# Expert 1's weight loads ahead of expert 2's transposing loads on one queue, and joins of an expert's planes tied behind VectorE's sums, in a fused attention and mixture-of-experts kernel

## The chip, the cores and the metric

The program runs on one core of one Trainium2 chip. The metric is the device time of one execution in microseconds (us), lower is better. The kernel before took 710.95 us, the median of three timed executions (710.29 to 711.34).

## What is computed

A gated linear recurrence over 768 steps (4 batches, 8 heads, head size 48) gives 3072 tokens of 384 numbers. A noisy gate picks two of eight experts for each token; an expert is two matrix products with a ReLU between them, weighted and added to the token's output row. All is in float32.

```python
def _moe_ref(x, w_gate, w_noise, noise, w1, w2):
    ...
    for e in range(E):                       # 8 experts
        for k in range(2):
            mask = top2[:, k] == e
            h = np.maximum(x[mask] @ w1[e], 0.0)                       # 384 -> 1024
            out[mask] += top2_w[mask, k, None] * (h @ w2[e])           # 1024 -> 384
```

## The kernel before, in words

The first 40% of the span is the attention, the gates and the dispatch of token rows to slots in DRAM (`xs`). The change lies behind that, in the experts, which run one after the other.

**One expert.** An expert has 832 slots, in two windows: window 0 with 320 rows (output blocks j = 0, 1, 2 of 128, 128 and 64 rows) and window 1 with 512 rows (blocks 3 to 6 of 128). Each float32 operand is held as two parts, high and low, and a product is three matmuls: high by high, high by low, low by high.

- `load_w1` and `load_w2` load the weights as three and four pieces into `raw` (three buffers, shared by both); ScalarE casts a piece to the high part (line 789), VectorE subtracts for the low part (line 790), and that frees the `raw` buffer.
- `load_x` loads the slots' rows into `xga` (window 0) and `xgb` (window 1); `x_G` takes the gate weights and the token numbers out of them.
- From expert 2 on, `x_P` splits the rows into 16-bit halves (ScalarE, line 754) and writes them to DRAM (`xp`, line 755); `x_L` reads them back with transposing DMAs (`xu`, line 763, six for a window); `x_T` joins the two halves of one of three planes again on VectorE (`xj`, line 828, the **join**), makes the high part on ScalarE (line 829) and the low part on VectorE (line 830). There are six joins for an expert, three for each window.
- `mm1` is the first product: eight blocks f for each window, nine matmuls each (line 842) into `ph`, which has four accumulator banks. ScalarE's ReLU gives the high part of `h` (line 844), VectorE the low part (line 847); in window 0 that is two instructions, of 256 and 64 columns. When both are done the bank is free.
- `mm2` is the second product: 24 matmuls for an output block (line 868; the 64-row block j = 2 has eight and eight, lines 873 and 876) into `po`, which has **two** accumulator banks. VectorE's **sum** (line 881) multiplies by the gate weight and adds into `ao`, and so frees the bank; a GpSimd DMA scatters `ao` to the output (line 882). `gather_o` fetches the output rows of the next expert into `ao`.

**What sets the order.** Up to the end of expert 1 each engine's and the sync queue's order (SP) is written out by hand in `ORDER`, tokens like `load_w21.2` (piece 2 of expert 1's second weights), `x_L2_0.3` (expert 2, window 0, transposing load 3), `mm21_1_4.0` (expert 1, output block 4: VectorE's sum) and `x_T2_1_0.0` and `.1` (expert 2, window 1, plane 0: join and low part). Of the experts from 2 on, the loop at the end emits the calls, and a scheduler places them on the engines by priority and its own estimate; SP's DMAs alone are held in the order of the calls. In the loop the joins of the next expert stand behind `mm2(e, 0)` and `mm2(e, 1)` in the text, and the scheduler may move them ahead:

```python
        mm2(e, 0)
        if e + 1 < E:
            for kk in range(KD):
                x_T(e + 1, 0, kk)
        mm2(e, 1)
```

Of the kernel before, what the change touches and what calls it, by code (L numbers as in the profile page):

```python
# [13 lines left out]
U16 = mybir.dt.uint16  # L14
I32 = mybir.dt.int32
AF = mybir.ActivationFunctionType
OP = mybir.AluOpType
# [198 lines left out]
        load_w12.2 mm20_1_4.0 load_w12.1 mm11_1_1.0 x_G2_0.1 x_G2_0.0 load_w21.0 mm20_1_5.0 mm11_1_0.0 mm20_1_6.0  # L216
        load_w21.1 load_w21.3 load_w21.2 mm11_1_2.0 mm11_1_3.0 mm11_1_4.0 mm11_1_5.0 mm21_0_0.0 mm11_1_6.0 mm21_0_1.0
        mm11_1_7.0 x_T2_0_0.0 x_T2_0_0.1 x_G2_1.0 x_G2_1.1 mm21_0_2.0 mm21_0_2.1 x_T2_0_1.0 x_T2_0_1.1 x_T2_0_2.0
        x_T2_0_2.1 mm21_1_3.0 x_T2_1_0.0 x_T2_1_0.1 x_T2_1_1.0 x_T2_1_1.1 x_T2_1_2.0 x_T2_1_2.1 mm21_1_4.0 mm21_1_5.0
        mm21_1_6.0  # L220
    """,
    "SP": """
        load_a0.0 load_a0.1 load_a1.0 load_a1.1 load_a2.0 load_a2.1 load_qk0.0 load_qk1.0 load_a3.1 load_qk2.0 p31.0
# [15 lines left out]
        load_v20.0 load_v21.0 load_v22.0 p322.1 load_w20.0 load_w20.1 load_w20.2 gscat3_0_4.0 gscat4_0_3.0 load_x1_0.0  # L239
        load_w20.3 load_v23.0 load_x1_0.1 load_w11.0 load_w11.1 load_w11.2 gscat4_3_4.0 load_w12.0 gscat5_3_4.0  # L240
        gscat5_0_3.0 load_x0_1.0 load_w12.1 load_w12.2 load_x1_1.0 load_x2_0.0 clear_out3.0 load_x2_0.1 load_w21.0
        load_w21.1 load_x2_1.0 x_P2_0.0 x_L2_0.0 x_L2_0.1 x_L2_0.2 x_L2_0.3 x_L2_0.4 x_L2_0.5 load_w21.2 load_w21.3
        x_P2_1.0 x_L2_1.0 x_L2_1.1 x_L2_1.2 x_L2_1.3 x_L2_1.4 x_L2_1.5
    """,
}
# [74 lines left out]
def kernel(  # L320
# [8 lines left out]
    nc = tc.nc  # L329
# [5 lines left out]
    N, DM = out.shape  # L335
    E = w_gate.shape[1]
    FF = w1.shape[2]
    KD = DM // 128
# [9 lines left out]
    JS = ((0, 1, 2), (3, 4, 5, 6))  # L348
# [396 lines left out]
        return d  # L745

    XU = {}

    def x_P(e, w):
        js = JS[w]  # L750
# [36 lines left out]
    order = mybir.DependencyInfo(mybir.DependencyClass.NoSync, mybir.DependencyReason.DATA)  # L787
# [28 lines left out]
    def x_T(e, w, kk):  # L816
        n = WIN[w][1]
        src_t = xga if w == 0 else xgb
        js = JS[w]
        x = XW[w, kk] = mt([128, 2, n], F32R, name=f"x{w}{kk}")  # L820
        if e < 2:
            p = ps_tile("px")
            for j in js:
                o = TO[j]
                nc.tensor.transpose(p[:, o:o + 128], src_t[:, j - js[0], kk * 128:(kk + 1) * 128], ident)
        else:
            p = mt([128, 512], F32, name="xj")
            nc.vector.tensor_copy(p[:, :n].bitcast(U16).rearrange("p (d two) -> p two d", two=2), XU[w, kk])  # L828
        nc.scalar.copy(x[:, 0, :], p[:, :n])  # L829
        nc.vector.tensor_tensor(x[:, 1, :], p[:, :n], x[:, 0, :].bitcast(F32), op=OP.subtract)  # L830

# [23 lines left out]
                in_offset=bass.IndirectOffsetOnAxis(ap=OX[e][0:w, j:j + 1], axis=0),  # L855
                bounds_check=N - 1, oob_is_err=False)

    osc = {}

    def mm2(e, w, js=None):  # L860
        for j in js or JS[w]:
            n, o = TW[j], TO[j]
            p = psO.tile([128, 512], F32, name="po")
            a, g = ao[j][0:n, :], GW[e][0:n, j:j + 1]
# [5 lines left out]
            else:  # L870
# [7 lines left out]
                lo = mt([n, DM], F32, name="lo")  # L878
                nc.scalar.copy(lo, p[n:2 * n, :DM])
                nc.vector.scalar_tensor_tensor(a, lo, g, a, op0=OP.mult, op1=OP.add)  # L880
            nc.vector.scalar_tensor_tensor(a, p[0:n, :DM], g, a, op0=OP.mult, op1=OP.add)  # L881
            d = nc.gpsimd.indirect_dma_start(  # L882
                out=out, out_offset=bass.IndirectOffsetOnAxis(ap=OX[e][0:n, j:j + 1], axis=0),
                in_=a, in_offset=None, bounds_check=N - 1, oob_is_err=False)
# [9 lines left out]
    for g in range(NG):  # L894
# [12 lines left out]
        for j in range(B):  # L907
            n = B * g + j
# [111 lines left out]

    emit([c for x in sorted(fill) for c in fill[x]])

    after = mybir.DependencyInfo(mybir.DependencyClass.NoSync, mybir.DependencyReason.DATA)
    for i, (first, *rest) in sorted(phases.items()):
        for x in rest:
            tc.add_manual_dep(x.ins, first.ins.name, after, reason="table")
# [108 lines left out]
    for e in range(2, E):  # L1135
        if e == 3:
            flag = flags()
            held.close()
        load_w2(e)
        gather_o(e)  # L1140
        mm1(e, 0)
        if e + 1 < E:
            load_x(e + 1, 0, xga)
            load_x(e + 1, 1, xgb)
        mm1(e, 1)
        if e + 1 < E:
            load_w1(e + 1)
            for w in range(2):
                x_G(e + 1, w)
                x_P(e + 1, w)  # L1150
            for w in range(2):
                x_L(e + 1, w)
        mm2(e, 0)
        if e + 1 < E:
            for kk in range(KD):
                x_T(e + 1, 0, kk)
        mm2(e, 1)
        if e + 1 < E:
            for kk in range(KD):
                x_T(e + 1, 1, kk)  # L1160
    nc.pop_inst_callback()
    mctx.close()

# [168 lines left out]
```

## Time and profile before

| what | value |
|---|---|
| timed executions | 710.95 us median of 3 (710.29 to 711.34) |
| the profiled execution | 705.07 us |
| its span (first to last instruction) | 703.4 us |
| TensorE matmul busy | 671.9 us, 96% of the span |
| VectorE busy | 438.2 us, 62% |
| ScalarE busy | 359.6 us, 51% |
| TensorE's mean granted clock | 0.99 of full speed |

PE is TensorE's matmuls, PEld its weight loads, DVE VectorE, ACT ScalarE, POOL GpSimd, SP the sync queue. The profiled execution is 5.9 us shorter than the median of the timed ones. The time that an engine waits stands in brackets behind the instruction that ended the wait, with what released it; a line of the windows view gives the engines' busy time in a stretch and the clock that TensorE was granted there.

### The profile page before, as it was taken

To read this page: it belongs to the slowest core of one execution; us is meant where nothing else is said; L and a number is where in the kernel's file an instruction comes from. 1 tells how busy PE (TensorE), PEld (TensorE's weight loads), DVE (VectorE), ACT (ScalarE), POOL (GpSimd) and SP (SyncE) were. 2 spreads that over 40 slices of the span, in tenths; PEclk is the share of its full clock that TensorE was granted. 3 is DMA by queue.
4 is the path that set the end of the run, shared out by engine and by line. 5 is a ranking of instruction groups with operands and counts; after the bars stand their busy time and mean duration, and the time that the engine had idled before them with its cause. 6 is when DMAs were issued, how large, how long until landed. Compare 5 with 4: busy or idle time off the path is not lost.

```text
span 703.4 us, 14277 instructions
## 1 busy us (share of the span) xinstructions
PE 671.9 (96%) x5532; PEld 591.5 (84%) x5535; DVE 438.2 (62%) x985; ACT 359.6 (51%) x597; POOL 176.4 (25%) x187
## 2 busy tenths in 40 slices
PE   7999999999999999996999899999999999999995
PEld 2477787888888998895998898898899899899895
DVE  7999999999987573513566445535627626644321
ACT  6899999989655423414265135217317307403200
POOL 3000000443453320333142124124123122323221
PEclk9999999999999999998999999999999999999998
DMA  6857667766787361355466448528617727632110
GB/s 228 257 163 186 190 186 250 193 218 198 230 284 244 135 240 47 118 171 163 133 213 196 126 138 248 150 81 275 166 61 268 165 100 256 157 118 76 42 39 31
DMA packets 101916, 118.52 MB, mean 168 GB/s; under 512 B 58738, under 2 KB 81115, under 8 KB 101840
## 3 DMA queue, kind: packets, MB, share of 16 engines
q1 hardware_dynamic: 92288, 89.98, 42.0%
q0 software_dynamic: 9552, 27.54, 12.0%
q8 instruction: 46, 0.75, 0.4%
q14 instruction: 30, 0.25, 0.1%
HBM read 70.91 MB, written 40.34 MB: 158 GB/s over the span
## 4 chain that ended last, share of the span: by engine, by line
PE 46%; DMA 12%; SPq 10%; DVE 10%; ACT 9%; issue 3%; POOL 0%; POOLq 0%; ACTq 0%; DVEq 0%
PE po L868 19%; SPq L763 9%; PE ph L842 8%; DMA xgb<-xs 4%; PE ptr L565 3%; DMA xu<-xp 3%; PE psc L575 2%; DMA xp<-xp 2%; PE pY L624 2%; ACT xp L754 2%; PE pY L626 2%; PE po L873 2%; PE po L876 2%; PE psc L842 2%; ACT w1h L789 1%
## 5 line engine op out<-in xcount | busy, mean ns | idle before, releaser
L868 PE MATMUL po<-w2h,h 128*128 128x384 f32 x768 | 200.3, 337 | 6.2 <-ACT w2h L789 6.2
L842 PE MATMUL ph<-x,w1h 128*128 128x512 f32 (+1 forms) x720 | 194.1, 354 | 0.4 <-DVE h L847 0.4
L868 PEld LDWEIGHTS po<-w2h,h 128*128 128x128 f32 x768 | 140.3, 189 | 7.5 <-ACT w2h L789 6.6
L842 PEld LDWEIGHTS ph<-x,w1h 128*128 128x128 f32 x720 | 127.8, 188 | 16.5 <-ACT h L844 0.8
L868 PE MATMUL po<-w2l,h 128*128 128x384 f32 x384 | 129.4, 337 | 0.3 <-DVE w2l L790 0.3
L842 PE MATMUL ph<-x,w1l 128*128 128x512 f32 (+1 forms) x360 | 127.3, 354 | 0.2 <-DVE w1l L790 0.2
L882 POOL DMA_INDIRECT out_dram<-ao,ox x56 | 56.8, 1014 | 276.0 <-DVE ao L881 228.4
L847 DVE SCALAR_TENSOR_TENSOR h<-ph,h 128x512 fp32r<-128x512 f32 (+2 forms) x176 | 73.9, 451 | 57.9 <-ACT h L844 57.7
L844 ACT ACTIVATE h<-ph 128x512 fp32r<-128x512 f32 (+1 forms) x120 | 62.0, 525 | 76.1 <-PE ph L842 66.1
L699 POOL DMA_INDIRECT xs<-xr,sl x48 | 54.1, 1127 | 180.1 <-DMA v<-in_v_dram 118.4
L881 DVE SCALAR_TENSOR_TENSOR ao<-po,gw,ao 128x384 f32<-128x384 f32 (+1 forms) x56 | 33.9, 611 | 76.1 <-PE po L868 75.2
L842 PEld LDWEIGHTS ph<-x,w1l 128*128 128x128 f32 x360 | 67.6, 188 | 8.6 <-DVE w1l L790 0.5
L868 PEld LDWEIGHTS po<-w2l,h 128*128 128x128 f32 x384 | 72.6, 189 | 1.1 <-DVE w2l L790 0.7
L789 ACT CAST w2h<-raw 128x768 fp32r<-128x768 f32 x32 | 26.6, 834 | 87.4 <-PE po L868 70.5
L853 POOL DMA_INDIRECT ao<-out_dram,ox x49 | 57.4, 1171 | 52.4 <-issue 34.8
L829 ACT CAST x<-xj 128x320 fp32r<-128x320 f32 (+1 forms) x36 | 19.5, 540 | 67.3 <-DVE xj L828 67.3
L790 DVE TENSOR_TENSOR w2l<-raw,w2h 128x768 fp32r<-128x768 f32 x32 | 30.3, 956 | 25.2 <-ACT w2h L789 24.5
L575 PEld LDWEIGHTS psc<-qT,kT 112*64 112x64 f32 x768 | 36.4, 137 | 6.7 <-issue 2.8
L575 PE MATMUL psc<-qT,kT 112*64 112x128 f32 (+1 forms) x768 | 40.1, 250 | 1.8 <-DVE h L847 1.4
L828 DVE COPY xj<-xu 128x640 uint16<-128x640 uint16 (+1 forms) x36 | 23.2, 644 | 23.3 <-DMA xu<-xp 22.9
L626 PE MATMUL pY<-am,v 128*48 128x128 f32 x384 | 36.3, 274 | 0.3
L576 DVE TENSOR_TENSOR am<-psc,mask 128x512 f32<-128x512 f32 x48 | 32.5, 682 | 3.0 <-PE psc L575 2.9
(218 smaller groups left out, 1012.9 us busy)
## 6 DMA issues: line engine op xcount, KB each, us to landing
raw<-in_moe_w_dram SPq DMA_DIRECT2D x24, 512.0 KB
raw<-in_moe_w_dram SPq DMA_DIRECT2D x32, 384.0 KB
qk<-in_qk_dram SPq DMA_DIRECT2D x24, 384.0 KB
v<-in_v_dram SPq DMA_DIRECT2D x24, 288.0 KB
xgb<-xs SPq DMA_DIRECT2D x8, 800.0 KB
re<-in_a_dram SPq DMA_DIRECT2D x12, 384.0 KB
im<-in_a_dram SPq DMA_DIRECT2D x12, 384.0 KB
out_dram<-none SPq DMA_DIRECT2D x12, 384.0 KB
```

The lines of the kernel that those rows point to most:

```text
L575: nc.tensor.matmul(p[o:o + 64, j, z:], KT[n][:, h, z:z + 64], QT[n][:, h, z:], start=True, stop=True, skip_group_check=True)
L626: nc.tensor.matmul(o, V[n][:, H + h // 2 if h % 2 else h, :], AM[n][:, h, :], start=not g, stop=True, skip_group_check=True)
L699: d = nc.gpsimd.indirect_dma_start(out=xs, out_offset=bass.IndirectOffsetOnAxis(ap=sl[:, kk, b:b + 1], axis=0), in_=XR[g][:, lo + b, :], i ...
L763: nc.sync.dma_start(x[:, i, :], xp[e % 2, lo:lo + n, i * DM + kk * 128:i * DM + (kk + 1) * 128], transpose=True)
L789: nc.scalar.copy(hi, raw_t)
L842: nc.tensor.matmul(p[:, :n], W1[e, kk][i][:, f * 128:(f + 1) * 128], XW[w, kk][:, j, :], start=(m == 0), stop=(m == len(ms) - 1))
L844: nc.scalar.activation(h[:, 0:n], p[:, :n], AF.Relu)
L847: nc.vector.scalar_tensor_tensor(h[:, dst:dst + b - a], p[:, a:b], 0.0, h[:, a:b].bitcast(F32), op0=OP.max, op1=OP.subtract)
L853: nc.gpsimd.indirect_dma_start(out=ao[j][0:w, :], out_offset=None, in_=out, in_offset=bass.IndirectOffsetOnAxis(ap=OX[e][0:w, j:j + 1], ax ...
L868: nc.tensor.matmul(p[:, :DM], HT[w, f][i][:, o:o + 128], W2[f // 2][k2][:, f % 2, :], start=(m == 0), stop=(m == len(ms) - 1))
L881: nc.vector.scalar_tensor_tensor(a, p[0:n, :DM], g, a, op0=OP.mult, op1=OP.add)
L882: d = nc.gpsimd.indirect_dma_start(out=out, out_offset=bass.IndirectOffsetOnAxis(ap=OX[e][0:n, j:j + 1], axis=0), in_=a, in_offset=None, b ...
```

## The change

Three orders change; no operation is added or taken away.

1. On SP, `load_w21.2` and `load_w21.3` stand ahead of the six transposing loads `x_L2_0`, no longer behind them.
2. On VectorE, in the table, the sums of expert 1's output blocks 4, 5 and 6 stand between the joins of expert 2's window 1, no longer behind all three.
3. In the loop, each join of expert e + 1 is tied behind the sum that was emitted last: the first two joins behind block 3, the next two behind block 4, one behind block 5, one behind block 6.

```diff
     "DVE":
-        x_T2_0_2.1 mm21_1_3.0 x_T2_1_0.0 x_T2_1_0.1 x_T2_1_1.0 x_T2_1_1.1 x_T2_1_2.0 x_T2_1_2.1 mm21_1_4.0 mm21_1_5.0
-        mm21_1_6.0
+        x_T2_0_2.1 mm21_1_3.0 mm21_1_4.0 x_T2_1_0.0 x_T2_1_0.1 mm21_1_5.0 x_T2_1_1.0 x_T2_1_1.1 mm21_1_6.0 x_T2_1_2.0
+        x_T2_1_2.1
     "SP":
-        load_w21.1 load_x2_1.0 x_P2_0.0 x_L2_0.0 x_L2_0.1 x_L2_0.2 x_L2_0.3 x_L2_0.4 x_L2_0.5 load_w21.2 load_w21.3
+        load_w21.1 load_x2_1.0 x_P2_0.0 load_w21.2 load_w21.3 x_L2_0.0 x_L2_0.1 x_L2_0.2 x_L2_0.3 x_L2_0.4 x_L2_0.5
     def x_T(e, w, kk):
...
-            nc.vector.tensor_copy(p[:, :n].bitcast(U16).rearrange("p (d two) -> p two d", two=2), XU[w, kk])
+            t = nc.vector.tensor_copy(p[:, :n].bitcast(U16).rearrange("p (d two) -> p two d", two=2), XU[w, kk])
+            if e > 2:
+                tc.add_manual_dep(t.ins, kept[-1].ins.name, after, reason="order")
     def mm2(e, w, js=None):
...
-            nc.vector.scalar_tensor_tensor(a, p[0:n, :DM], g, a, op0=OP.mult, op1=OP.add)
+            kept.append(nc.vector.scalar_tensor_tensor(a, p[0:n, :DM], g, a, op0=OP.mult, op1=OP.add))
     for e in range(2, E):
...
         mm2(e, 0)
-        if e + 1 < E:
-            for kk in range(KD):
-                x_T(e + 1, 0, kk)
-        mm2(e, 1)
-        if e + 1 < E:
-            for kk in range(KD):
-                x_T(e + 1, 1, kk)
+        for j in JS[1]:
+            mm2(e, 1, (j,))
+            if e + 1 < E:
+                for w, kk in {3: ((0, 0), (0, 1)), 4: ((0, 2), (1, 0)), 5: ((1, 1),), 6: ((1, 2),)}[j]:
+                    x_T(e + 1, w, kk)
```

What the scheduler makes of it, in the changed program (its line numbers are one to three higher).

VectorE at the end of expert 3 (`xj` is a join, `x` the low part behind it, `ao` a sum, `h` the low part of an `mm1` block). Before, from the middle of `mm1` on:

```order
L828 COPY xj<-xu_5663 128x2x512
L847 SCALAR_TENSOR_TENSOR h_5593<-ph,h_5593 128x512
L830 TENSOR_TENSOR x_5885<-xj,x_5885 128x512
L828 COPY xj<-xu_5666 128x2x512
L847 SCALAR_TENSOR_TENSOR h_5606<-ph,h_5606 128x512
L830 TENSOR_TENSOR x_5890<-xj,x_5890 128x512
L828 COPY xj<-xu_5669 128x2x512
L830 TENSOR_TENSOR x_5895<-xj,x_5895 128x512
L881 SCALAR_TENSOR_TENSOR ao_3871<-po,gw,ao_3871 128x384
L881 SCALAR_TENSOR_TENSOR ao_3872<-po,gw,ao_3872 128x384
```

The same joins in the changed program, from the sum of block 5 on, with what follows them at the start of expert 4:

```order
L884 SCALAR_TENSOR_TENSOR ao_3876<-po,gw,ao_3876 128x384
L829 COPY xj<-xu_5666 128x2x512
L791 TENSOR_TENSOR w2l_5903<-raw,w2h_5902 128x768
L833 TENSOR_TENSOR x_5861<-xj,x_5861 128x512
L791 TENSOR_TENSOR w2l_5909<-raw,w2h_5908 128x768
L884 SCALAR_TENSOR_TENSOR ao_3877<-po,gw,ao_3877 128x384
L829 COPY xj<-xu_5669 128x2x512
L791 TENSOR_TENSOR w2l_5915<-raw,w2h_5914 128x768
L850 SCALAR_TENSOR_TENSOR h_5945<-ph,h_5945 128x256
L833 TENSOR_TENSOR x_5895<-xj,x_5895 128x512
L791 TENSOR_TENSOR w2l_5921<-raw,w2h_5920 128x768
L850 SCALAR_TENSOR_TENSOR h_5945<-ph,h_5945 128x64
```

All six joins stood ahead of the sum of block 0; now none does. The last join and the fourth subtraction for the second weights stand ahead of the second part of block 0's low part (`h`, 64 columns), which frees an accumulator bank of `ph`.

TensorE in window 0 of expert 2's `mm1`, in the changed program, behind the fourth of eight blocks (`po` are matmuls of expert 2's second product, for output blocks 0 and 1):

```order
L845 MATMUL ph<-x_4628,w1h_4227 128x320 x2
L845 MATMUL ph<-x_4628,w1l_4228 128x320
L871 MATMUL po<-w2h_4790,h_4833 128x384
L871 MATMUL po<-w2l_4791,h_4833 128x384
L871 MATMUL po<-w2h_4790,h_4833 128x384
L871 MATMUL po<-w2l_4791,h_4833 128x384
L871 MATMUL po<-w2h_4790,h_4833 128x384
L845 MATMUL ph<-x_4618,w1h_4215 128x320 x2
```

Before, these five matmuls stood behind all sixteen blocks of `mm1`. In the later experts TensorE's order is as before.

## Rows read from the trace of the kernel before

**Rows 1.** The page: TensorE's granted clock in 40 slices, in tenths of full speed.

```profile
PEclk9999999999999999998999999999999999999998
```

**Rows 2.** Waits of TensorE from 280 us on: total, times, longest.

```profile
PE po L868 <- ACT w2h L789: 6.2, 1, 6.2
PE po L873 <- DVE ao L881: 4.9, 5, 2.4
```

**Rows 3.** Windows at TensorE's waits and two clean ones: length, then busy time by engine.

```profile
315.56:328.66 13.10, 6.56 (x25) 5.84 (x25) 5.18 (x7) 7.17 (x11) 4.97 (x5) 0.74 0.48 144
330.74:334.91 4.17, 4.17 (x25) 4.17 (x25) 0.69 (x1) 0.60 (x1) 0.00 (x0) 1.00 0.51 157
392.42:399.41 6.99, 4.61 (x17) 3.88 (x18) 2.93 (x5) 0.62 (x1) 2.03 (x2) 0.76 0.71 238
451.66:455.73 4.07, 3.06 (x17) 2.73 (x18) 1.48 (x3) 0.00 (x0) 2.03 (x2) 1.00 0.52 190
508.74:511.99 3.25, 3.06 (x17) 2.73 (x18) 0.66 (x2) 0.00 (x0) 2.03 (x2) 1.00 0.46 166
563.94:567.68 3.74, 3.09 (x18) 2.76 (x18) 1.12 (x3) 0.00 (x0) 2.04 (x2) 1.00 0.50 187
620.05:623.76 3.71, 3.07 (x17) 2.74 (x18) 1.11 (x3) 0.00 (x0) 2.03 (x2) 1.00 0.51 187
675.70:678.50 2.80, 2.80 (x18) 2.47 (x17) 0.62 (x1) 0.00 (x0) 1.00 (x1) 1.00 0.12 46
```

**Rows 4.** Windows behind two waits: the number after five busy times is the granted clock.

```profile
322.83:327.32 4.49, 4.18 (x12) 3.78 (x13) 4.23 (x6) 4.49 (x8) 0.00 (x0) 0.50 0.10 35
...
394.80:399.00 4.20, 4.20 (x15) 3.52 (x16) 1.29 (x2) 0.16 (x1) 2.03 (x2) 0.59 0.76 277
```

**Rows 5.** Timeline of the sync queue around expert 1's second weights.

```profile
305.75 8.81 SPq L763 DMA_TRANSPOSE xu<-xp  x6
314.67 1.03 SPq L803 DMA_DIRECT2D raw<-in_moe_w_dram  x2
```

**Rows 6.** Timeline of ScalarE at the same place.

```profile
321.22 1.56 ACT L789 CAST w2h<-raw 128x768 fp32r<-128x768 f32 x2 [15.14 <-DMA raw<-in_moe_w_dram]
```

**Rows 7.** Timeline of VectorE: expert 1's weights, and joins ahead of a sum.

```profile
306.11 0.96 DVE L790 TENSOR_TENSOR w2l<-raw,w2h 128x768 fp32r<-128x768 f32 x1 [0.37 <-ACT w2h L789]
...
393.51 0.74 DVE L828 COPY xj<-xu 128x1024 uint16<-128x1024 uint16 x1 [0.69 <-DMA xu<-xp]
394.14 0.60 DVE L881 SCALAR_TENSOR_TENSOR ao<-po,gw,ao 128x384 f32<-128x384 f32 x1
```

**Rows 8.** Timelines of VectorE, the sync queue and ScalarE where expert 4 begins.

```profile
470.23 3.04 DVE L790 TENSOR_TENSOR w2l<-raw,w2h 128x768 fp32r<-128x768 f32 x3 [1.33 <-ACT w2h L789]
473.18 0.61 DVE L881 SCALAR_TENSOR_TENSOR ao<-po,gw,ao 128x384 f32<-128x384 f32 x1
474.28 0.56 DVE L847 SCALAR_TENSOR_TENSOR h<-ph,h 128x256 fp32r<-128x256 f32 x2 [0.49 <-ACT h L844]
...
471.21 0.37 SPq L803 DMA_DIRECT2D raw<-in_moe_w_dram  x1
...
473.81 0.44 ACT L844 ACTIVATE h<-ph 128x320 fp32r<-128x320 f32 x1 [1.54 <-PE ph L842]
474.64 0.84 ACT L789 CAST w2h<-raw 128x768 fp32r<-128x768 f32 x1 [0.39 <-DMA raw<-in_moe_w_dram]
```

**Rows 9.** ScalarE's ReLU of two blocks in a row, window 0 of expert 7.

```profile
644.48 0.44 ACT L844 ACTIVATE h<-ph 128x320 fp32r<-128x320 f32 x1 [0.70 <-PE ph L842]
645.80 0.44 ACT L844 ACTIVATE h<-ph 128x320 fp32r<-128x320 f32 x1 [0.88 <-PE ph L842]
```

**Rows 10.** VectorE: a join, its low part, and expert 1's last sum.

```profile
349.49 0.75 DVE L828 COPY xj<-xu 128x1024 uint16<-128x1024 uint16 x1
350.99 0.69 DVE L830 TENSOR_TENSOR x<-xj,x 128x512 fp32r<-128x512 f32 x1 [0.74 <-ACT x L829]
...
356.76 0.62 DVE L881 SCALAR_TENSOR_TENSOR ao<-po,gw,ao 128x384 f32<-128x384 f32 x1 [3.81 <-PE po L868]
```

More of the change, by code (lines that the diff above doesn't have):

```diff
@@ L747 @@
     XU = {}
+    after = mybir.DependencyInfo(mybir.DependencyClass.NoSync, mybir.DependencyReason.DATA)
     def x_P(e, w):
@@ L856, in gather_o @@
                 bounds_check=N - 1, oob_is_err=False)
-    osc = {}
+    osc, kept = {}, []
     def mm2(e, w, js=None):
@@ L1021 @@
     emit([c for x in sorted(fill) for c in fill[x]])
-    after = mybir.DependencyInfo(mybir.DependencyClass.NoSync, mybir.DependencyReason.DATA)
     for i, (first, *rest) in sorted(phases.items()):
```

## The prediction

> **What bounds the kernel now.** I read the page first. TensorE's matmuls fill 96% of the span (the table of the profile), and its granted clock is full but for one slice and the last [rows 1]. So the kernel is bound by TensorE, and an order can only give back time in which TensorE waits or runs at the lower clock. Next come the waits of TensorE behind 280 us [rows 2]. There are two kinds that matter: one wait of 6.2 us of the second product (L868) for ScalarE's cast of `w2h`, and five waits, 4.9 us in all and 2.4 at the longest, of the 64-row block (L873) for VectorE's sum. Then the windows view prices them [rows 3]. A block of 24 matmuls takes 4.17 us when nothing disturbs it (second line); the one at 315.56 took 13.10. The 64-row block takes 2.80 us in expert 7, which has no joins beside it (last line); in experts 2 to 6 it took 6.99, 4.07, 3.25, 3.74 and 3.71, counted from the end of the block before. The reader is to see two things in these lines: the time over the clean one, and the granted clock (the number ahead of the last two), which is 0.74 and 0.76 in the two long ones. Behind the 6.2 us wait TensorE ran at 0.50 of its clock for 4.49 us, that is at 1.2 GHz of 2.4, and behind the 2.4 us wait the mean was 0.59 over 4.2 us [rows 4]. So a long wait is paid for twice, and a wait of 1 us (451.66, clock 1.00) once.
>
> **Who causes them.** Timelines of the other engines answer that. The transposing loads hold the sync queue from 305.75 to 314.56, and only then the two last pieces of expert 1's second weights are issued [rows 5]. ScalarE had waited 15.14 us for them when it went on at 321.22 [rows 6]; its order has piece 3 ahead of piece 1, so TensorE lacked piece 1, which had long landed. Piece 3 needs the `raw` buffer of piece 0, which VectorE frees at 306.11 + 0.96 = 307.07 [rows 7]. The five other waits come from a join at the head of VectorE's queue: at 393.51 it had waited for a transposing load, and the sum that frees the accumulator bank ran only behind it, at 394.14 [rows 7].
>
> **Part 1, the weight loads on SP.** Pieces 2 and 3 are now ahead of six transposing loads. Piece 2 can leave at once, piece 3 at 307.1. How long it takes to land is the unknown. Expert 4's fourth piece was issued at 471.21 and was there when ScalarE took it at 474.64: 3.4 us [rows 8]. The two pieces at 314.67, issued behind the transposes and with each other, took 6.5 to ScalarE's start at 321.22 [rows 5, 6]. With 3.4, piece 3 is there at 310.5, with 6.5 at 313.6. Two casts of 0.8 and a subtraction of 0.96 lie between that and the matmuls that need piece 1: 313.1 or 316.2. TensorE reaches them at 315.56 + 6 x 0.17 = 316.6. Either way it does not wait, and the whole excess goes, the lower clock with it: 13.10 - 4.17 = **8.93 us**. I take 3.4, since the transposes are now behind the load. The low end is a load that lands only when the transposes are through, at 314.6 + 3.4 = 318.0: TensorE then waits 318.0 + 2.6 - 316.6 = 4.0 and runs slowly for a while (2 us more, from 4.49 us at half clock), so 2.9 us are left.
>
> The rule that bears on this is in the Trainium skill, DMA: Bandwidth & Descriptors, section "Issuing engines are not separate DMA queues": all DMAs run on the same 16 engines and interleave. Read strictly, being first in the queue does not protect piece 3 from the transposes issued right behind it, and the sum would tend to the low end, 6.0 us less gain. The rows here do not decide it, since no weight load in them has transposes behind it.
>
> The transposes start at 307.6 rather than 305.75 and end some 2 us later. Their join of window 0 comes behind all of expert 1's first product; in the trace nothing waited for them there, so this costs nothing. If that cover went, it would cost those 2 us at most.
>
> **Part 2, the table's sums.** Expert 1's sums no longer stand behind joins, for which I count nothing. But the last join now comes behind the last sum, at 356.76 + 0.62 = 357.4, and takes 350.99 + 0.69 - 349.49 = 2.19 us with its pass through ScalarE [rows 10]. Expert 2's three weight subtractions of 0.96 follow [rows 7], three small operations that I put at 0.3 together, and block 0's low part, 0.56 as in expert 4 [rows 8]: done at 363.3, or some 0.3 sooner, since neighbours overlap a little. TensorE starts expert 2 at about 356.6 and needs that bank after four blocks of 1.32 us [rows 9], at 361.9. The five matmuls that the scheduler moved there fill about 0.7 us before they need the same low part. That leaves a new wait of **0.5 us** (none, if the ReLU and the casts come sooner; 1.5, if the casts on ScalarE queue up behind the join).
>
> **Part 3, the joins in the loop.** The joins go behind the sums of blocks 3 to 6, so the sums of blocks 0 and 1 meet an empty queue. The excess of the five 64-row blocks goes [rows 3]: 4.19 + 1.27 + 0.45 + 0.94 + 0.91 = **7.76 us**. The low bound is 4: if each kept 0.75.
>
> What is late next is the start of the next expert, which now has the last two joins in it. I work it out at expert 4, where the three subtractions started at 470.23 [rows 8]. VectorE now does: subtraction to 471.2, low part of a join 471.9, subtraction 472.8, the last sum 473.3, the last join 474.1, subtraction 475.0, 256 columns of block 0 475.4, the join's low part 476.1, the fourth subtraction 477.0, the 64 columns 477.2. TensorE needs that bank after four blocks: the first ReLU was at 473.81, and three more blocks of 1.32 end at 477.8, less some 0.2 us for ScalarE's start, 477.6. So 0.4 us is left. The fourth subtraction, which stood behind block 0 before, needs the fourth piece, which is issued behind the first subtraction at 471.2 and landed by 474.64. I take 0.1 us for each of five starts, **0.5 us**; bounds are 0 and 1 us each. The planes themselves are in time: window 0's last one is made behind block 4's sum, two blocks of 4.17 us before TensorE wants it, and window 1's last one is wanted 8 x 1.32 = 10.6 us into the expert.
>
> The sync queue gets its `raw` buffers at the same places, and the transposing loads of the next expert stay where they are, so that the joins, now some 10 us later, find them landed. Five sums less wait behind joins also start GpSimd's scatters earlier, on an engine that TensorE does not wait for.
>
> **The sum.** 8.93 + 7.76 - 0.5 - 0.5 = 15.7 us less. The profiled execution, 705.07 us with a span of 703.4, would take 689.4. It was 5.9 us shorter than the median of the timed runs; I take the same difference off that median: 710.95 - 15.7 = **695.3 us**.
>
> **Rivals.**
> - *The load lands late* (part 1's low end): 6 us less gain, 701.3 us; with half of it, 698. For it: the skill's rule. Against it: 3.4 us in expert 4, with other loads issued right behind. Chance 0.08.
> - *The starts of the experts give it back in part*: VectorE's queue is a microsecond longer there than I worked out, at five starts, 4.5 us: 699.8. For it: only 0.4 us is left. Against it: every duration is from a row. Chance 0.08.
> - *Slower than before*: the same place, but long enough for the clock. The fourth piece's subtraction now stands ahead of the bank's release, so a late landing stops TensorE in its fifth block. If the piece took over 7 us instead of 3.4, TensorE would wait about 2.4 us at each of five starts, which is the shortest wait behind which the lower clock was seen, and lose 4.19 - 2.39 = 1.8 more to the clock: 4.2 x 5 = 21, so 716. Against it: ScalarE waited 0.39 us for this piece at that place. Chance 0.03.
> - *The ties do nothing*: the sum of block 0 is late for some other reason, such as the fetched rows of `ao`, and only part 1 remains: 710.95 - 8.93 + 1 = 703.0. Against it: the chain of waits goes through the join. That neither part works, 711, I hold for less likely still. Chances 0.03 and 0.02.
>
> **How the numbers follow.** The forecast has 0.76. Its own range is 693.5 to 697; the lower end takes both new costs as nothing, and half a microsecond for the spread of the runs. Reaching to the two partial rivals gives 693 to 701.5, with 0.08 left out. No change means within 0.2%, or 1.4 us, about what a measurement of this kernel can tell. Faster: 0.76 + 0.08 + 0.08 + 0.03 = 0.95; same 0.02; slower 0.03.
>
> **What would show it.** TensorE's waits for `w2h` and for `ao` in L868 and L873 (now L871 and L876) should be gone, the block at 315.6 should take 4.2 us, the five 64-row blocks 2.8, and the granted clock stay full behind 300 us. ScalarE's 15 us wait for `raw` should be about 4. I am wrong if TensorE now waits for VectorE's `h` in the fifth block of window 0, or if piece 3 of expert 1 still lands behind 314 us.

## The result and the profile after

The changed kernel took 692.76 us (median of four runs, 691.3 to 693.51), the kernel before on the same chip 710.62 (709.69 to 711.34): a ratio of 0.9747 with a 95% interval of 0.9727 to 0.9767, or 17.9 us. The forecast was 695.3 with a range of 693.0 to 701.5. The direction and the mechanism came as forecast; the time lies 2.5 us below the forecast and 0.24 below the range. The profiled execution after is the one of 693.51 us, with a span of 691.8.

The page's clock line, against [rows 1]: full but for the last slice. A digit stands for a slice of 17 us and 9 for 90% or more, so a few microseconds at the lower clock can hide in it, as the second stretch of [rows 4] does in [rows 1].

```profile
PEclk9999999999999999999999999999999999999998
```

Waits of TensorE from 280 us on (total, times, longest), against [rows 2]. Both kinds of wait that the prediction named are gone. The view lists waits over 0.15 us, and one of 0.3 us is left:

```profile
PE ph L845 <- DVE h L850: 0.3, 1, 0.3
```

Windows of after, against [rows 3]: block 0 of expert 1's second product, then the 64-row blocks of experts 2 to 7, each from the end of the block before. Columns: stretch, length, busy time of PE, PEld, DVE, ACT and POOL, granted clock, DMA share, GB/s.

```profile
320.64:324.81 4.17, 4.17 (x25) 4.17 (x25) 1.73 (x3) 4.01 (x6) 3.25 (x4) 1.00 0.60 151
388.58:391.38 2.80, 2.80 (x18) 2.47 (x17) 0.62 (x1) 0.00 (x0) 1.00 (x1) 1.00 0.61 133
443.65:446.45 2.80, 2.80 (x17) 2.47 (x17) 0.62 (x1) 0.00 (x0) 1.00 (x1) 1.00 0.73 277
499.65:502.45 2.80, 2.80 (x17) 2.47 (x17) 0.62 (x1) 0.00 (x0) 1.00 (x1) 1.00 0.80 289
554.39:557.19 2.80, 2.80 (x18) 2.47 (x17) 0.62 (x1) 0.00 (x0) 1.00 (x1) 1.00 0.94 355
609.57:612.37 2.80, 2.80 (x17) 2.47 (x17) 0.62 (x1) 0.00 (x0) 1.00 (x1) 1.00 0.73 273
664.31:667.11 2.80, 2.80 (x18) 2.47 (x17) 0.62 (x1) 0.00 (x0) 1.00 (x1) 1.00 0.11 43
```

Every block has its clean length and the full clock. Block 0 went from 13.10 to 4.17 us, the five 64-row blocks from 21.76 in all to 14.00.

How piece 3 went, in the timelines of the sync queue, VectorE and ScalarE of after, against [rows 5 to 7]. Everything is 5.08 us later here than before, since the attention part of this execution was that much longer (told below):

```profile
304.05 8.50 SPq L804 DMA_DIRECT2D raw<-in_moe_w_dram  x2
312.98 8.17 SPq L764 DMA_TRANSPOSE xu<-xp  x6
...
311.19 0.96 DVE L791 TENSOR_TENSOR w2l<-raw,w2h 128x768 fp32r<-128x768 f32 x1 [0.37 <-ACT w2h L790]
...
315.58 1.57 ACT L790 CAST w2h<-raw 128x768 fp32r<-128x768 f32 x2 [4.42 <-DMA raw<-in_moe_w_dram]
```

VectorE frees the `raw` buffer at 311.19 + 0.96 = 312.15, piece 3 leaves then (the second of the two loads in the first row), six transposing loads follow at 312.98, and ScalarE casts it at 315.58: 3.4 us, as taken. ScalarE's wait is 4.4 us instead of 15.1.

The start of expert 4 on VectorE, from the last sum of expert 3 on, and ScalarE's first ReLU (last row), against [rows 8]:

```profile
463.29 0.61 DVE L884 SCALAR_TENSOR_TENSOR ao<-po,gw,ao 128x384 f32<-128x384 f32 x1
463.82 0.75 DVE L829 COPY xj<-xu 128x1024 uint16<-128x1024 uint16 x1
464.45 0.94 DVE L791 TENSOR_TENSOR w2l<-raw,w2h 128x768 fp32r<-128x768 f32 x1
465.31 0.42 DVE L850 SCALAR_TENSOR_TENSOR h<-ph,h 128x256 fp32r<-128x256 f32 x1
465.65 0.68 DVE L833 TENSOR_TENSOR x<-xj,x 128x512 fp32r<-128x512 f32 x1
466.25 0.95 DVE L791 TENSOR_TENSOR w2l<-raw,w2h 128x768 fp32r<-128x768 f32 x1
467.12 1.14 DVE L850 SCALAR_TENSOR_TENSOR h<-ph,h 128x64 fp32r<-128x64 f32 x5
...
464.53 0.44 ACT L847 ACTIVATE h<-ph 128x320 fp32r<-128x320 f32 x1 [1.54 <-PE ph L845]
```

The order is the one that the prediction walked through. The 64 columns of block 0 begin at 467.12 and take 0.2 us. TensorE wants the bank at 464.53 + 3 x 1.32 - 0.2 = 468.3, about 1 us later: the slack is there, and larger than the 0.4 us worked out.

For what follows I divide an execution in two. The *attention part* ends at the first matmul of block 0 of expert 1; the *expert part* goes from there to the end of the last matmul. The attention part went from 315.40 to 320.48 us, the expert part from 379.77 to 363.31, a gain of 16.5.

### The profile page after: what moved, and what is told of

The parts are those of the page before. It is cut to its first block, busy times and chain, and to the rows that moved or that the text cites. A ratio compares the mean times of both kernels' runs of the same rounds, so it can differ in the third digit from the quotient of the medians.

```text
span 691.8 us, 14256 instructions
## 1 busy us (share of the span) xinstructions
PE 669.8 (97%) x5535; PEld 590.8 (85%) x5535; DVE 435.6 (63%) x985; ACT 360.1 (52%) x597; POOL 177.0 (26%) x187
## 4 chain that ended last, share of the span: by engine, by line
PE 70%; DVE 12%; DMA 3%; ACT 3%; issue 1%; another core or an unknown queue 1%; SPq 1%; POOL 0%; POOLq 0%; DVEq 0%; ACTq 0%
PE ph L845 28%; PE po L871 27%; PE psc L575 2%; PE ptr L565 2%; PE pY L624 2%; DVE am L576 2%; PE psc L845 2%; PE po L879 1%; PE po L876 1%; PE pY L626 1%; DMA xgb<-xs 1%; DMA ecol<-es 1%; DVE kh L555 1%; DVE w1l L791 1%; DVE qk L547 1%
## 5 line engine op out<-in xcount | busy, mean ns | idle before, releaser
L885 POOL DMA_INDIRECT out_dram<-ao,ox x56 | 59.0, 1054 | 259.4 <-DVE ao L884 214.1
L699 POOL DMA_INDIRECT xs<-xr,sl x48 | 51.9, 1082 | 187.6 <-DMA car<-tf 119.3
L882 ACT COPY lo<-po 64x384 f32<-64x384 f32 x8 | 3.8, 478 | 63.0 <-PE po L879 63.0
```

Of the source, the lines that this page charges most:

```text
L699: d = nc.gpsimd.indirect_dma_start(out=xs, out_offset=bass.IndirectOffsetOnAxis(ap=sl[:, kk, b:b + 1], axis=0), in_=XR[g][:, lo + b, :], i ...
L885: d = nc.gpsimd.indirect_dma_start(out=out, out_offset=bass.IndirectOffsetOnAxis(ap=OX[e][0:n, j:j + 1], axis=0), in_=a, in_offset=None, b ...
```

## The experiments

**Each part alone.** e1_sp has only the sync queue's order, e2_loop only the loop, e3_sp_loop both without the table's sums.

```diff
--- before
+++ e1_sp
-        load_w21.1 load_x2_1.0 x_P2_0.0 x_L2_0.0 x_L2_0.1 x_L2_0.2 x_L2_0.3 x_L2_0.4 x_L2_0.5 load_w21.2 load_w21.3
+        load_w21.1 load_x2_1.0 x_P2_0.0 load_w21.2 load_w21.3 x_L2_0.0 x_L2_0.1 x_L2_0.2 x_L2_0.3 x_L2_0.4 x_L2_0.5
--- after
+++ e2_loop
-        load_w21.1 load_x2_1.0 x_P2_0.0 load_w21.2 load_w21.3 x_L2_0.0 x_L2_0.1 x_L2_0.2 x_L2_0.3 x_L2_0.4 x_L2_0.5
+        load_w21.1 load_x2_1.0 x_P2_0.0 x_L2_0.0 x_L2_0.1 x_L2_0.2 x_L2_0.3 x_L2_0.4 x_L2_0.5 load_w21.2 load_w21.3
--- after
+++ e2_loop, e3_sp_loop
-        x_T2_0_2.1 mm21_1_3.0 mm21_1_4.0 x_T2_1_0.0 x_T2_1_0.1 mm21_1_5.0 x_T2_1_1.0 x_T2_1_1.1 mm21_1_6.0 x_T2_1_2.0
-        x_T2_1_2.1
+        x_T2_0_2.1 mm21_1_3.0 x_T2_1_0.0 x_T2_1_0.1 x_T2_1_1.0 x_T2_1_1.1 x_T2_1_2.0 x_T2_1_2.1 mm21_1_4.0 mm21_1_5.0
+        mm21_1_6.0
```

> Only part 1 (the sync queue's order); the joins and sums stay as before. The expert part is counted from the first matmul of expert 1's block 0 to the end of the last matmul: 379.77 us before, 363.31 after. My terms are independent: TensorE's wait for w2h goes with its slow clock, 8.9 us, and the five waits of the 64-row blocks stay (4.9 us in all, excess 7.8). Expert part 370.9, time about 701.8. Rival, the parts overlap (the half clock behind the 6.2 us wait or a later hole pays for part of it): less than 7 or more than 10.5 us. For the 1.4 us that the timed gain (17.9) has over the gain of the expert part (16.5): if the execution of before that was profiled was a short one in its attention part, this one's attention part is near 320.5, not 315.4; if the sync queue's order makes the difference, e1_sp has it and e2_loop does not.

> Only part 3 (joins tied behind sums in the loop); the sync queue and the table as before. By my terms the five 64-row blocks fall to 2.8 us each (7.8 us less), TensorE still waits 6.2 us for w2h and runs at half clock behind it, and the starts of experts 3 to 7 cost 0 to 0.2 us: expert part 372.0 to 372.3, time about 703. Rival, the starts cost what I had put down (0.1 each and more): above 372.5, and waits of L845 for DVE h in the fifth block of window 0. Attention part near 320.5 if the execution profiled of before was a short one; near 315.4 if it is the sync queue's order that makes it longer.

> Parts 1 and 3 without the table's sums (part 2). Part 2 was put at nothing for expert 1's blocks and 0.5 us lost at the start of expert 2; the trace of after shows 0.27 gained at expert 1's block 6 and 0.28 lost at the start of expert 2. If those two belong to part 2, here the start of expert 2 is 0.28 shorter and expert 1's last block 0.27 longer than in after, and the expert part is 363.3 again (363.0 to 363.6), time as after within 0.2%. Rival: the five matmuls that the scheduler moved hide a wait of 0.5 us or more, and the expert part is over 363.8 without them or under 362.9.

Measured beside before at 703.42 us: e1_sp 695.42 (ratio 0.9868, 0.9829 to 0.9908), e2_loop 696.64 (0.9897, 0.9864 to 0.9931), e3_sp_loop 688.0 (0.977, 0.9737 to 0.9804): 8.0, 6.8 and 15.4 us. TensorE's waits behind 280 us, first in e1_sp and then in e2_loop, show that each part takes away its own kind and leaves the other:

```profile
PE po L873 <- DVE ao L881: 5.7, 5, 2.4
```

```profile
PE po L871 <- ACT w2h L790: 6.2, 1, 6.2
```

The parts add up: 8.0 + 6.8 = 14.8 against 15.4 together. The times expected there start from 710 us for before and cannot be compared; the expert parts can. That of e1_sp was 372.8, not 370.9. Its five 64-row blocks took 8.2 us over their clean length, where the first trace of before had 7.8 and e4_before, from the same chip, 6.4; the larger part of the miss, about 1.5 us, lies in the first products of experts 3, 4 and 6, two thirds of it at expert 4, where TensorE waits for VectorE's `h` and ScalarE's 16-bit copies. That spread is followed up below. The expert part of e2_loop, 371.2, was even below its range, so no cost of the starts shows. In e3_sp_loop it was 364.3, by number in the range of its rival, but not for the rival's reason: 1.1 us are waits behind VectorE's `h` in later experts. Against a1_after, expert 1 took 0.27 us longer there up to its last block and the start of expert 2 was 0.29 shorter, as expected: the table's sums give back what they take, and no timing can tell them.

**What a load costs behind and among transposes.** f1_mid puts piece 3 behind three of the six transposing loads, f2_last behind all six.

```diff
--- after
+++ f1_mid
-        load_w21.1 load_x2_1.0 x_P2_0.0 load_w21.2 load_w21.3 x_L2_0.0 x_L2_0.1 x_L2_0.2 x_L2_0.3 x_L2_0.4 x_L2_0.5
+        load_w21.1 load_x2_1.0 x_P2_0.0 load_w21.2 x_L2_0.0 x_L2_0.1 x_L2_0.2 load_w21.3 x_L2_0.3 x_L2_0.4 x_L2_0.5
--- after
+++ f2_last
+        load_w21.1 load_x2_1.0 x_P2_0.0 load_w21.2 x_L2_0.0 x_L2_0.1 x_L2_0.2 x_L2_0.3 x_L2_0.4 x_L2_0.5 load_w21.3
```

> The changed kernel, but piece 3 of expert 1's second weights stands behind three of the six transposing loads instead of ahead of all. With S the start of block 0 of expert 1: in after piece 3 was issued at S - 8.3 and ScalarE cast it at S - 4.9, 3.4 us later, with six transposes issued right behind it. Theory (the place in the queue decides when it leaves, and then it takes 3.4): three transposes of 1.4 from S - 9.6, issue at S - 5.5, cast at S - 2.1, half a microsecond before TensorE would lack piece 1; no wait, expert part as in after, 363.3 to 364.3. Rival (the transposes around it slow it to the 6.5 us seen in before): cast at S + 1.0, a wait of TensorE for w2h of 2.6 us and about 2 more at half clock, expert part 367 to 368.5.

> The changed kernel, but piece 3 alone stands behind all six transposing loads (piece 2 stays ahead). In before both pieces left there, at S - 0.7, and took 6.5 us to ScalarE's start. Theory A (6.5 was the price of two loads at once): piece 3 alone takes 3.4, cast at S + 2.6, TensorE waits about 3.0 us and runs at half clock behind it, block 0 takes about 9.5 instead of 13.1. Theory B (6.5 was the price of transposes still in flight): cast at S + 5.8, TensorE waits 6.2 us as before, block 0 takes 13.1, expert part 372.

The load on the sync queue and ScalarE's cast of it, in the timelines of f1_mid and then of f2_last:

```profile
310.66 0.52 SPq L804 DMA_DIRECT2D raw<-in_moe_w_dram  x1
...
314.48 1.57 ACT L790 CAST w2h<-raw 128x768 fp32r<-128x768 f32 x2 [8.20 <-DMA raw<-in_moe_w_dram]
```

```profile
313.62 0.58 SPq L804 DMA_DIRECT2D raw<-in_moe_w_dram  x1
...
318.03 1.56 ACT L790 CAST w2h<-raw 128x768 fp32r<-128x768 f32 x2 [12.74 <-DMA raw<-in_moe_w_dram]
```

And TensorE's waits for these weights, in the same order:

```profile
PE po L871 <- DVE w2l L791: 0.4, 1, 0.4
```

```profile
PE po L871 <- ACT w2h L790: 3.8, 1, 3.8
```

From issue to cast piece 3 took 3.4 us ahead of the transposes in after, 3.8 in their middle and 4.4 alone behind all six. In before, as the second load of the pair behind all six, it left at 315.23 and was cast at 321.22, 6.0 us later (the 6.5 of [rows 5, 6] count from the first load's issue). One trace each does not make the small steps sure: in the nine traces with piece 3 ahead of the transposes it took 3.4 to 3.6 us in eight, but 4.4 in f5_block, as much as behind all six. So the 0.4 and 1.0 us that transposes in flight seem to add are not clear of the spread. What a second load adds is larger: 5.6 to 6.2 us in the six traces with the pair, against 4.4 in f2_last.

Neither theory was quite right in f2_last (3.0 or 6.2 us of waiting forecast, 3.8 measured), the first was nearer. Its expert part was 370.6 us and its time 695.07. f1_mid's were 363.6 and 688.95, in the theory's range, though with a wait of 0.4 us where none was forecast. The step of part 1 holds with a margin: even from the middle block 0 took 5.4 us, 1.1 more than in after.

**The slower rival, made by hand.** f5_block puts three joins behind the last sum and ties the low part of the next expert's first block behind the last of them; f6_all does that for the first four blocks, so that no bank comes free earlier.

```diff
--- after
+++ f5_block
-                for w, kk in {3: ((0, 0), (0, 1)), 4: ((0, 2), (1, 0)), 5: ((1, 1),), 6: ((1, 2),)}[j]:
+                for w, kk in {3: ((0, 0), (0, 1)), 4: ((0, 2),), 5: (), 6: ((1, 0), (1, 1), (1, 2))}[j]:
...
+                    if e > 2 and w == 0 and f == 0:
+                        tc.add_manual_dep(t.ins, low[-1].ins.name, after, reason="order")
--- f5_block
+++ f6_all
-                    if e > 2 and w == 0 and f == 0:
+                    if e > 2 and w == 0 and f < 4:
```

> The changed kernel with three joins instead of one behind the last sum, and the low part of the next expert's first block tied behind the last join's low part: the rival on which the change would have been slower, made by hand. In after, block 0's low part was done 0.9 us before TensorE wanted the bank (467.3 against 468.3 at expert 4). Two more joins and low parts of 1.4 us each on VectorE, the passes through ScalarE between them and block 1's and 2's low parts that now run first: block 0's bank comes free 3 to 5 us later, TensorE waits 2 to 4 us in the fifth block of experts 3 to 7, 10 to 20 us, and where the wait is over 2.4 us the clock falls to half, 2 us more each: expert part 375 to 392. Rival (the start of an expert has more slack than I worked out, or the scheduler's order elsewhere hides it): under 366.

> As f5_block, but the low parts of all of the next expert's first four blocks are tied behind the last join's low part, so that no accumulator bank comes free before it (in f5_block TensorE took block 1's bank first and waited 0.3 to 0.6 us only). From f5_block's trace at expert 4: three joins with their passes through ScalarE take 2.1 us each behind the last sum at 460.0, so the last low part is done at 466.5, or at 469.2 where the copies of gate weights between them wait for the rows; block 0's low part 0.7 later; TensorE wants the bank at 463.7. Theory of the prediction's slower rival: waits of 3 to 6 us at five starts and half clock behind each, 2 to 3.5 us more: 25 to 48 us, expert part 387 to 411, slower than before. Rival: TensorE finds other work to do there and loses under 10 us.

TensorE's waits behind 300 us in f5_block and in f6_all:

```profile
PE ph L847 <- DVE h L852: 2.1, 5, 0.6
```

```profile
PE po L875 <- DVE h L852: 23.2, 5, 5.6
```

f5_block was a miss: 691.04 us, an expert part of 366.7, only 3.4 more than after, in place of 10 to 20. In its order VectorE makes block 1's low part ahead of block 0's, and at expert 4 TensorE's fifth block went on behind that, 5 us ahead of block 0's low part. f6_all took 722.63 beside before at 705.35, with an expert part of 398.3 (387 to 411 expected): five waits of 3.4 to 5.6 us, and the lower clock behind each. In its VectorE timeline at the start of expert 4 the bank's release stands behind joins, and these behind a copy that waits for rows:

```profile
470.88 0.17 DVE L814 COPY gw<-xga 128x3 f32<-128x3 f32 x1 [1.96 <-DMA xga<-xs]
...
474.74 0.69 DVE L833 TENSOR_TENSOR x<-xj,x 128x512 fp32r<-128x512 f32 x1 [0.73 <-ACT x L832]
475.35 1.93 DVE L852 SCALAR_TENSOR_TENSOR h<-ph,h 128x256 fp32r<-128x256 f32 x8
```

So the rival's mechanism exists and is slower than before, but it takes three joins and four tied blocks. The change with its one join is far from it.

**Where the last 2.5 us are.** Unchanged copies: e4_before, b2_before, b3_before and b4_before are before, a1_after and a2_after the changed kernel.

> The kernel before once more, for a second profile. Theory: its profiled execution of 705.07 us was a short one in the attention part; this one takes 710 to 711.3 with an attention part near 320.5 and an expert part of 379.5 to 380.1. Rival: the expert part of before varies from execution to execution (the lower clock behind its waits of 1 to 2.4 us comes or does not), so that it is 381 or more here.

> The changed kernel once more, for a second profile and its times beside before on this chip. Its gain over before was 17.9 us where both were timed first, against 16.5 us in the expert part of the two traces and 15.7 forecast; before alone was 710.6 us there and 703.4 on another chip. Theory: what differs is the attention part of the execution (320.5 us to block 0 of expert 1 in after's profile, 314.5 to 316.2 in all others), so that here the expert part is 363.3 to 364.3 again, the attention part 315 to 316.5 where before is near 703 and near 320 where it is near 710, and the gain 15 to 16.5 us. Rival: the attention part is longer in the changed kernel itself, near 320.5 here too.

> The kernel before, a third profile. Where its executions differ by up to 6 us on one chip (702.2 to 708.1), theory: it is the waits that hang on when a DMA has landed, the five 64-row blocks (excess over 2.8 us each: 7.8 in the first trace, 6.4 in the second) and the lower clock behind them, so that an expert part between 377 and 381 goes with an excess between 6 and 9 us, and the attention part stays within 1 us of 315.5. Rival: the expert part is within 0.5 us of 378 to 380 and the attention part varies by the microseconds.

> The kernel before, a fourth profile, as for b2_before: between the two, the difference in time is the difference of the five 64-row blocks and of waits for loaded rows at the starts (theory), or of the attention part (rival).

> The changed kernel, a third profile. Open is whether the 5.1 us that its first trace took longer up to block 0 of expert 1 (320.5 us against 315.1 to 316.2 in seven other traces) belong to that execution and chip. Theory: yes; attention part 315 to 316.5 where before is near 703 to 706, expert part 362.4 to 363.4, time 686.5 to 689.8, ratio 0.973 to 0.979. Rival: the kernel's own executions go both ways on one chip, so that here it is near 320.5, or that its four times spread over 5 us.

> The kernel before, a fifth profile. On the chip where before takes 709 to 714 us the changed kernel gained 20.4 us, where it takes 702 to 708 it gained 18.5, and the traces so far account for 15.3 to 18.9 in the experts. Theory: on a chip with the longer times the attention part is 320.5 us with TensorE's wait of 2.0 us at 202 us, as in the changed kernel's traces there, and the expert part is 381 to 384, since before has waits on landed DMAs that the changed kernel lacks; on the other kind of chip 315.1 to 316.2 and 377.6 to 381.3 as in the four traces so far. Rival: an expert part of 379 also where before takes 710 or more, the rest in the attention part (321 or over).

All in microseconds. Block 0 is counted here from its first matmul, 0.16 us ahead of the windows above; the excess is that of the five 64-row blocks over 2.80 each:

| trace | time | attention part | block 0 | excess | expert part |
|---|---|---|---|---|---|
| before, shown ahead | 705.07 | 315.40 | 13.26 | 7.8 | 379.77 |
| e4_before | 702.64 | 315.79 | 13.02 | 6.4 | 377.64 |
| b2_before | 706.94 | 315.87 | 13.57 | 8.4 | 381.32 |
| b3_before | 703.08 | 315.07 | 12.99 | 7.7 | 378.80 |
| b4_before | 712.71 | 319.52 | 14.03 | 9.5 | 383.98 |
| after | 693.51 | 320.48 | 4.33 | 0.0 | 363.31 |
| a1_after | 688.21 | 316.09 | 4.33 | 0.0 | 362.46 |
| a2_after | 692.28 | 320.59 | 4.33 | 0.0 | 362.48 |

The traces fall into two kinds, by chip; what the chips differ in no run shows. The execution shown ahead has the attention part of the first kind, the timed runs of before beside it the times of the second. On one kind before takes 702 to 708 and after 687.8 (a1_after, ratio 0.9756, 0.9705 to 0.9807); on the other before takes 709 to 714 and after 692.27 (a2_after, 0.9722, 0.9684 to 0.976). On the second kind the attention part is 4 to 5 us longer with either kernel. The new order on the sync queue is not what lengthens it: e1_sp and e3_sp_loop have that order and 316.2 and 316.1 us on the first kind. The theory of e4_before missed (702.64 us and 315.79, not 710 and 320.5). TensorE's waits in the attention part of all four traces of the second kind (after, a2_after, g2_rows, b4_before) have one that every other trace has at 0.3 us:

```profile
PE cum L634 <- DVE lz L653: 2.0, 1, 2.0
```

In three of the four it is followed by a stretch at a lower clock, here in the windows of after:

```profile
202.20:204.19 1.99, 0.00 (x1) 0.01 (x1) 0.23 (x2) 1.61 (x2) 0.89 (x1) 1.00 0.96 313
204.19:208.60 4.41, 4.41 (x41) 4.12 (x42) 4.31 (x12) 2.22 (x6) 0.97 (x1) 0.62 0.95 348
```

In b4_before the same wait took 2.01 us and the clock stayed at 1.00 over the 4.41 us behind it; its attention part is the shortest of the four. VectorE's copy at the end of the wait, in the timeline of after:

```profile
203.92 0.21 DVE L653 COPY lz<-cum 128x48 f32<-128x48 f32 x1 [3.75 <-remote]
```

Why it comes late the trace does not tell: VectorE stood idle for 3.75 us before it, and the releaser is none that the profile has. The change does not touch it.

In b4_before, the one trace of before on the second kind, the experts lose more as well. The transposing loads landed later against VectorE's order, and TensorE's longest wait for a sum was 4.2 us instead of 2.4. Waits of TensorE behind 280 us:

```profile
PE po L868 <- ACT w2h L789: 6.2, 1, 6.2
PE po L873 <- DVE ao L881: 6.1, 3, 4.2
PE ph L842 <- DVE h L847: 0.8, 3, 0.3
```

The first of three joins ahead of that sum on VectorE, in the timeline; in [rows 7] a join had waited 0.69 us:

```profile
396.40 0.76 DVE L828 COPY xj<-xu 128x1024 uint16<-128x1024 uint16 x1 [2.50 <-DMA xu<-xp]
```

In the changed kernel the joins wait for nothing, and its expert part is 362.5 to 363.3 on both kinds. So between the traces of the first kind the gain is 16 us (their mean for before without the one shown ahead, 704.2, less 688.2), and between those of the second 20.4 (712.71 - 692.28): 21.5 gained in the experts, 1.1 lost in the attention part. That the gain is larger on the second kind rests on this one trace. By the medians it is 18.5 us on a1_after's chip (15 to 16.5 were expected) and 20.4 on a2_after's, and the intervals of the two ratios overlap; before's seven runs on a1_after's chip alone spread over 5.5 us.

b2_before and b3_before, from one chip, differ by 3.9 us: 2.5 in the expert part, 0.8 in the attention part and 0.5 behind the last matmul, so the theory holds in the main. The rival of b2_before and a1_after, that the kernels' own attention parts vary by microseconds, fell: on the first kind they are within 315.1 and 316.2 in every trace but e2_loop (314.5), f2_last (314.6) and f6_all (314.9).

**What is left at the starts.** The small waits of e3_sp_loop and after come after copies of gate weights that wait for the next expert's rows; that the rows cause them is argued from the order, not shown. g1_rows issues the rows ahead of all second weights, g2_rows ahead of their fourth piece, with the copies tied to their old place.

```diff
--- after
+++ g1_rows
+        if e + 1 < E:
+            load_x(e + 1, 0, xga)
+            load_x(e + 1, 1, xgb)
         load_w2(e)
         gather_o(e)
         mm1(e, 0)
-        if e + 1 < E:
-            load_x(e + 1, 0, xga)
-            load_x(e + 1, 1, xgb)
--- after
+++ g2_rows
         for f2 in range(KF // 2):
+            if rows and f2 == 3:
+                load_x(e + 1, 0, xga)
+                load_x(e + 1, 1, xgb)
...
+                tc.add_manual_dep(t.ins, lowh[e - 1, 0, 2].ins.name, after, reason="order")
...
+                tc.add_manual_dep(c.ins, relu[e - 1, 0, 2].ins.name, after, reason="order")
```

> The changed kernel, with the loads of the next expert's rows (xga, xgb) issued ahead of the second weights' pieces on the sync queue instead of behind them. In two of four traces of the new order TensorE still waits 0.3 to 1.1 us in the experts, each time behind VectorE's copies of gate weights that wait for these rows. Theory: those waits go, the expert part is 362.3 to 362.6 in each execution, at most 1.1 us less and on a median 0.5, which the timed runs cannot tell from no change (within 0.2% of a1_after's 687.8 if before is near 706, ratio 0.972 to 0.977). Rival: the rows loaded earlier make the scheduler move ScalarE's 16-bit copies, and a new wait for ScalarE or a later weight piece costs 1 us or more.

> The changed kernel, with the next expert's rows loaded on the sync queue ahead of the fourth piece of the second weights (not ahead of all four, as g1_rows had them), and the copies that read them tied behind block 2 of window 0 on VectorE and ScalarE, so that they can't be moved to where the rows are still missing. Theory: the waits of 0.3 to 1.1 us behind the late rows go and nothing else comes; expert part 362.3 to 362.6, time within 0.2% of a2_after. Rival: the scheduler now puts the subtraction for the next first weights ahead of a block's low part at the start of an expert, where its piece has not landed; TensorE then waits 1 to 3 us at each of five starts, 5 to 20 us more with the lower clock.

g1_rows took 733.66 us (ratio 1.0397, 1.0363 to 1.0432), 28 more than before and the largest miss here. The sync queue and VectorE in the first product of expert 3:

```profile
426.07 16.18 SPq L764 DMA_TRANSPOSE xu<-xp  x12
442.30 0.58 SPq L736 DMA_DIRECT2D xga<-xs  x1
...
446.71 0.17 DVE L814 COPY gw<-xga 128x3 f32<-128x3 f32 x1 [13.48 <-DMA xga<-xs]
```

The scheduler moved the copy into the middle of that product, ahead of low parts, as if the rows were there early. The loads still stood behind twelve transposing loads, VectorE waited 13.5 us at the head of its queue, and TensorE 8.6 to 9.4 us in four experts. It is the mistake that the change itself mends, in a new place. g2_rows took 693.74 us (0.9746, 0.9707 to 0.9784) beside a2_after's 692.27: no better, with one wait of 0.4 us and an expert part of 363.5. None of these runs points to a version that beats the changed kernel: a1_after and a2_after have no listed wait of TensorE in their experts at all.

## Why the prediction was right, and where it was not

- **Part 1.** Right to the digit: 13.10 to 4.17, 8.93 us. Piece 3 left when its buffer came free, took 3.4 us, and TensorE did not wait; the lower clock went too. The rule named there, from the Trainium skill, DMA: Bandwidth & Descriptors, section "Issuing engines are not separate DMA queues", says that DMAs started by the scalar, sync or GpSimd engine run on the same 16 DMA engines and interleave. That transposes issued behind a load would therefore slow it was the prediction's own reading, and it did not come: 3.4 to 3.6 us in eight of nine traces, as in expert 4 before. A second weight load beside it did slow it, 5.6 to 6.2 us against 4.4.
- **Part 3's gain.** Right: all five blocks at 2.80, 7.76 us.
- **Where that was luck.** Both gains are right to the digit because they are compared with the trace on which they were sized. In the four other traces of before block 0 loses 8.7 to 9.7 us and the five blocks lose 6.4 to 9.5.
- **The new costs.** Taken too high. I put 0.5 us at the start of expert 2 and 0.5 at the five others. The pair of traces shows 0.28 and 0.21, and 0.27 gained at expert 1's last block, for which I had counted nothing: 0.2 net for 1.0. The 0.21 is hardly the change's: nearly all of it is at expert 4, where after loses 0.8 us and before 0.6, and a1_after, a2_after and e4_before lose nothing. At expert 4 the walk was half a microsecond too slow, since neighbours on VectorE overlap by about 0.1 us each, which I had allowed for at expert 2 only.
- **From the profiled execution to the median: the step that failed.** "It was 5.9 us shorter than the median of the timed runs; I take the same difference off that median" sizes the gain on one execution of before and treats the other 5.9 us as a constant beside the change. For most of them that was right: 5.1 us are a longer attention part that the changed kernel has as well. The rest is no constant, since a longer execution of before can also lose more in the very waits that are to go. b4_before, at 712.71 us, has an expert part 4.2 us longer than the trace the gain was sized on, 2.5 of it in block 0 (14.03 for 13.26) and in the 64-row blocks (9.5 for 7.8), while the changed kernel's expert part is 362.5 to 363.3 us on either kind of chip. So 15.7 us were too little for the runs they were taken off: 17.9 came there, and 20.4 on a2_after's chip. Most of the rest of the 4.2 us is in first products, where TensorE waits for VectorE's `h`; the changed kernel has some of that too (0.3 us of waiting in after). How much before lost in its experts in the timed runs of the forecast stays open, since none of them was traced; the sum of the miss leaves 0.8 us for it.
- **The sum of the miss.** Forecast 695.3, measured 692.76. From the pair of traces: 0.8 because the experts gained 16.5 and not 15.7, 0.2 from a shorter end, 0.8 from the difference above, and 0.75 because the profiled execution after is the longest of its four (its 0.8 us at expert 4 would account for that). The low end had room for both costs at nothing and half a microsecond of spread. That makes 693.8; 693.5 and then 693 were written without a further reason. There was no room for a gain beyond the one trace, and one kernel's runs on that chip spread over 2.2 us.
- **The rivals.** None occurred. The load did not land late: it was cast at 315.58, 4.9 us ahead of block 0, and f1_mid shows that a later place costs little. The ties did their part: e2_loop, which has nothing else, has all five 64-row blocks at 2.80. The slower one needs f6_all.

## What to carry to other kernels

A wait at the head of an in-order queue costs whatever stands behind it: ask of each instruction that waits for a DMA what frees a buffer behind it, and put that first, as the joins behind the sums here and not as the copies in g1_rows. When the profiled execution is shorter than the timed runs, don't carry the difference over as a constant: part of it may be the very waits that are to go. Where a gain is a wait that hangs on a landing DMA, size it on several traces, and let the range hold the spread of runs for both kernels.

## What the runs showed of the hardware

- Chips differ by a few microseconds in the same program, repeatably: the wait of 2.0 us at 202 us and an attention part near 320 us came in all four traces from the slower kind and in none of the others.
- The clock fell behind waits shorter than the 2.39 us that I had taken as the shortest: behind 1.99 us in after (0.62 over the next 4.41 us, above) and behind 2.00 us in e4_before. But the length of the wait alone does not settle it: behind 2.01 us in b4_before the clock stayed full, and behind 1.74 us in b3_before, on the 64-row block of expert 3, as well:

```profile
450.90:452.64 1.74, 0.00 (x1) 0.00 (x1) 1.28 (x3) 0.43 (x1) 0.00 (x0) 1.00 1.06 358
452.64:455.70 3.06, 3.06 (x17) 2.73 (x18) 0.47 (x1) 0.00 (x0) 2.03 (x2) 1.00 0.42 156
```

- A weight load of 384 KB issued right behind another took 5.6 to 6.2 us from issue to cast in six traces, with six transposing loads ahead of both; alone in that place it took 4.4 (f2_last, one trace). With the transposes behind it, it took 3.4 to 3.6 in eight traces and 4.4 in one.
